# Norms of double-precision weights: sums of squares on ScalarE, or products of the leading halves on TensorE

## The chip, the cores and the metric

The kernel runs on one NeuronCore of one Trainium2 chip. A time is the device time of one execution in microseconds (us); the median of three runs of the kernel before is 1164.04 us (1164.0 to 1165.47). The trace is from one profiled execution of 1164.36 us, whose span is 1162.6 us. Engines are named as the profile names them: PE is TensorE (PEld its weight loads), DVE is VectorE, ACT is ScalarE, POOL is GpSimd, SP is the engine that issues the DMAs.

## The reference

Attention with a threshold (batch 8, 8 heads, 576 rows, head size 64), then a feed-forward layer (512 to 2048 to 512) on the 4608 rows that come out:

```python
scores = (q @ k.T) / sqrt(64)
scores = where(scores >= max(scores) - tau, scores, -1e9)
x = softmax(scores) @ v                  # heads side by side: 4608 x 512
h = x @ w_in                             # 512 x 2048
g = s * relu(h)**2 + b
out = g @ w_out                          # 2048 x 512
```

The weights `w_in` and `w_out` reach the kernel as 8-byte floats, seen as pairs of 32-bit words.

## The kernel before

**The stages.** The first image is done by 36 "plain" tiles of 128 query rows (`plain_tile`, L444): 4-byte scores on PE (L457), row maximum (L460, DVE), exponential (L464, ACT), mask and sum (L466, DVE), reciprocal (L471, DVE), a product on POOL (L472), transposes on PE (L480), a copy on ACT (L484), products with `v` on PE (L493). The other seven images are done by "split" tiles, in which each operand is held as a high and a low 2-byte piece (`split_tile`, L500; `with_v`, L540, products at L547). The feed-forward layer runs in blocks of 256 rows, each of 16 steps f, one for each 128 of the 2048 hidden columns: products with `w_in` (L756), relu, square and pieces on ACT (L760, L763, L764), the low piece on POOL (L765), products with `w_out` (L771). `sums` (L685) adds up `w_out` for the bias.

**The weights.** They are cut into 16 tiles f of `w_in` (`iw`, u = 0) and 16 of `w_out` (`ow`, u = 1), 512 KB each. `load_weights` (L561) issues their DMAs on SP. `weights(f)` (L573) then makes an approximate 4-byte float of the upper word: a Prelu on ACT (L589) and a shift on DVE (L592). From that it takes norms. For `w_in`: ACT squares the tile into a 2-byte scratch (L594), PE multiplies the squares with a matrix of ones into 128 columns of bank `h` (`sizes`, L599), DVE takes the maximum of the columns (L601). For `w_out`: ACT squares the tile and accumulates each row's sum (L603, which shows in a trace as an ACTIVATE and a READ_ACCUMULATOR). `weight_scales` (L607) makes powers of two from all 32 results: two reductions (L610, L612), a product with ones on PE (L615), short DVE steps (L617 to L624), one on POOL (L627), which writes `wpower`.

Only with `wpower` can a weight be cut into its high piece (L653, ACT) and low piece (L658, DVE), which the feed-forward steps multiply. Before that, `whole` (L645, DVE) joins the two words of a tile into one 4-byte float in place; it needs no `wpower`, but overwrites what the norms read.

**The order.** No order is written by hand. Every operation is given to a planner (`Plan`) with an engine, an occupancy, a latency and the keys that it reads and writes; `place` puts them out as a list scheduler, `run` repeats that backward and forward and keeps the shortest, and the instructions are issued on each engine in the planned order. So a changed operation or a changed cost can change the order everywhere. The costs that the change touches are those of the weights' DMAs (L567, L570) and of `with_v` (L549). `keep_busy` (L898) adds filler products to the first 12 tiles, which write columns 256 to 511 of bank `h` (L901) and have their own key, `idle`.

Of the kernel before, what the change touches and what calls it, by code (L numbers as in the profile page):

```python
# [9 lines left out]
F32 = mybir.dt.float32  # L10
# [3 lines left out]
AF = mybir.ActivationFunctionType  # L14
# [126 lines left out]
def tile_attention_ffn(ctx: ExitStack, tc: tile.TileContext, qT, kT, v, tau, w_in, w_out, s, b, out):  # L141
# [25 lines left out]
    def const(name, shape, dt=F32):  # L167
        return cp.tile(shape, dt, name=name)
# [11 lines left out]
    vm = const("vm", [P, 2], F32R)  # L180
    norm = [const(f"norm{i}", [P, 4]) for i in range(2)]
    power = [const(f"power{i}", [P, 5, 4]) for i in range(2)]
    wmost, wnorm, wpower, wback = const("wmost", [P, 2, NF]), const("wnorm", [P, 4]), const("wpower", [P, 4, 2]), const("wback", [P, 2])
    ones16, onesb = const("ones16", [P, P], F16), const("onesb", [P, P], BF16)
    vs = [const(f"vs{i}", [P, 4]) for i in range(2)]
    vt = [const(f"v{i}", [P, 5, P], F16) for i in range(3)]
    rk, rq, rv = const("rk", [P, 2, S]), const("rq", [P, 2, S]), const("rv", [P, 2, 5, D])
# [7 lines left out]
    def early(tag):  # L195
        if tag not in lazy:
            lazy[tag] = sb(tag, [P, 9 * S // 2], F32)
        return lazy[tag]
# [341 lines left out]
    def with_v(g, at):  # L540
        ps = bank["pv"][:, 0:g.n]
        slots = [(n, u) for n in range(9) for u in range(2 if n < 5 else 1)]

        def products():
            for i, (n, u) in enumerate(slots):
                for j, hd in enumerate(g.hds):
                    nc.tensor.matmul(ps[j * D:(j + 1) * D], hd.v[:, (n + 1) % 5, u * D:(u + 1) * D],  # L547
                                     lazy[("ea", "eb")[j]][:, n, g.c0:g.c0 + g.n], start=(i == 0), stop=(i == len(slots) - 1))
        cost = len(slots) * (0.42 * g.n + 8) + 300  # L549
        plan.add("PE", (cost, cost + 170), products, g.keys + [k for hd in g.hds for k in hd.kvs], ["pv"], at)  # L550
        hd = g.hds[0]
        for off, n, dest, key in g.dests:
            kx = [key + (j, u) for j in range(2) for u in range(2)] if key[0] == "x" else [key + (j,) for j in range(2)]
            act((105 + 1.04 * n, 203 + 1.04 * n), lambda off=off, n=n, dest=dest: nc.scalar.activation(
                out=dest, in_=ps[:, off:off + n], func=AF.Copy, scale=hd.unit), ["pv", hd.kunit], kx, at)
# [5 lines left out]
    def load_weights(f, at):  # L561

        def raw(u):
            if ("raw", f, u) not in lazy:
                lazy["raw", f, u] = sb("io"[u] + f"w{f}", [P, DM, 2], I32)
            return lazy["raw", f, u]
        plan.add("SP", (1800, 6700), lambda: nc.sync.dma_start(out=raw(0).rearrange("p (c f) t -> p c (f t)", c=NC),  # L567
                                           in_=w_in.rearrange("(c p) (n g) -> n p c g", p=P, n=NF)[f]),
            [], [(f"w{f}", "i")], at)
        plan.add("SP", (1800, 6700), lambda: nc.sync.dma_start(out=raw(1).rearrange("p f t -> p (f t)"),  # L570
                                           in_=w_out[f * P:(f + 1) * P, :]), [], [(f"w{f}", "o")], at)

    def weights(f, at):  # L573

        tag = f"t{f % 2}"  # L580

        def words(k, u):
            return lazy["raw", f, u][:, :, k]

        def squares():
            return early("eb")[:, 2 * DM * (f % 2):2 * DM * (f % 2) + DM // 2].bitcast(BF16)
        for u, k in (0, "i"), (1, "o"):
            kr = f"w{f}", k
            act((563, 667), lambda u=u: nc.scalar.activation(  # L589
                out=words(1, u).bitcast(F32), in_=words(1, u).bitcast(F32), func=AF.Prelu, scale=2.0 ** -112, alpha=-2.0 ** 32),  # L590
                [kr], [kr], at)
            dve2((328, 418), lambda u=u: nc.vector.tensor_scalar(  # L592
                out=words(1, u), in0=words(1, u), scalar1=3, scalar2=None, op0=ALU.logical_shift_left), [kr], [kr], at)
        act((563, 667), lambda: nc.scalar.activation(out=squares(), in_=words(1, 0).bitcast(F32), func=AF.Square),  # L594
            [(f"w{f}", "i")], [tag], at)

        def sizes():
            for c in range(NC):
                nc.tensor.matmul(bank["h"][:, 0:P], onesb, squares()[:, c * P:(c + 1) * P], start=(c == 0), stop=(c == NC - 1))  # L599
        pe(NC, P, sizes, [tag, "ones16"], ["h"], at)  # L600
        dve((200, 290), lambda: nc.vector.tensor_reduce(  # L601
            out=wmost[:, 0, f:f + 1], in_=bank["h"][:, 0:P], axis=mybir.AxisListType.X, op=ALU.max), ["h"], [("wmost", 0, f)], at)
        act((640, 860), lambda: nc.scalar.activation(  # L603
            out=early("eb")[:, 2 * DM * (f % 2) + DM // 2:2 * DM * (f % 2) + DM].bitcast(BF16), in_=words(1, 1).bitcast(F32),
            func=AF.Square, accum_out=wmost[:, 1, f:f + 1]), [(f"w{f}", "o")], [("wmost", 1, f), (tag, 1)], at)

    def weight_scales(at):  # L607

        most = [("wmost", u, f) for u in range(2) for f in range(NF)]
        dve((90, 170), lambda: nc.vector.tensor_reduce(  # L610
            out=wnorm[:, 0:2], in_=wmost, axis=mybir.AxisListType.X, op=ALU.max), most, ["wnorm"], at)
        dve((90, 170), lambda: nc.vector.tensor_reduce(  # L612
            out=wnorm[:, 2:3], in_=wmost[:, 1], axis=mybir.AxisListType.X, op=ALU.add), most, [("wnorm", 2)], at)
        top = bank["pv"][:, 384:386]
        pe(1, 64, lambda: nc.tensor.matmul(top, ones.bitcast(F32), wnorm[:, 2:4], start=True, stop=True),  # L615
           ["ones", "wnorm", ("wnorm", 2)], [("top", 384)], at)
        dve((72, 155), lambda: nc.vector.tensor_scalar(  # L617
            out=wpower[:, 0, 0:1], in0=wnorm[:, 0:1], scalar1=LEAST, scalar2=None, op0=ALU.max), ["wnorm"], ["wpower"], at)
        dve((72, 155), lambda: nc.vector.tensor_scalar(
            out=wpower[:, 0, 1:2], in0=top[:, 0:1], scalar1=LEAST, scalar2=None, op0=ALU.max), [("top", 384)], ["wpower"], at)  # L620
        dve((72, 155), lambda: nc.vector.tensor_scalar(
            out=wpower.bitcast(I32)[:, 1], in0=wpower.bitcast(I32)[:, 0], scalar1=1, scalar2=EXPONENT,
            op0=ALU.logical_shift_right, op1=ALU.bitwise_and), ["wpower"], ["wpower"], at)
        dve((72, 155), lambda: nc.vector.tensor_scalar(  # L624
            out=wpower.bitcast(I32)[:, 2], in0=wpower.bitcast(I32)[:, 1], scalar1=EXPONENT, scalar2=None,
            op0=ALU.bitwise_xor), ["wpower"], ["wpower"], at)
        pool((270, 195), lambda: nc.gpsimd.tensor_scalar(  # L627
            out=wpower[:, 2], in0=wpower[:, 2], scalar1=UP, scalar2=1.0, op0=ALU.mult, op1=ALU.mult), ["wpower"], ["wpower"], at)

        def back():  # L630
            g = nc.gpsimd
            g.tensor_scalar(out=wpower[:, 3], in0=wpower[:, 1], scalar1=DOWN, scalar2=1.0, op0=ALU.mult, op1=ALU.mult)
            g.tensor_tensor(out=wback[:, 0:1], in0=s_t, in1=wpower[:, 3, 0:1], op=ALU.mult)
            g.tensor_tensor(out=wback[:, 1:2], in0=b_t, in1=wpower[:, 3, 1:2], op=ALU.mult)
            g.tensor_tensor(out=wback[:, 0:1], in0=wback[:, 0:1], in1=wpower[:, 3, 1:2], op=ALU.mult)
            g.tensor_tensor(out=wback[:, 0:1], in0=wback[:, 0:1], in1=wpower[:, 3, 0:1], op=ALU.mult)
            g.tensor_scalar(out=wback[:, 0:1], in0=wback[:, 0:1], scalar1=H_DOWN ** -2, scalar2=1.0, op0=ALU.mult, op1=ALU.mult)
        pool((1800, 1800), back, ["wpower", "s_", "b"], ["wback"], at + 1)
# [252 lines left out]
    def zeros():  # L891
        nc.gpsimd.memset(ones.bitcast(F32), 1.0)
        nc.gpsimd.memset(qt.bitcast(F32), 0.0)
        nc.gpsimd.memset(ones16, 1.0)
        nc.gpsimd.memset(onesb, 1.0)
    pool((700, 700), zeros, [], ["ones", "qt0", "qt1", "ones16"], -10)

    def keep_busy(n, r):  # L898
# [10 lines left out]
    pool((700, 700), constants, [], ["ident", "qd0", "qd1"], -9)  # L909

    def bounds():
        for t in [vm.bitcast(F32), wnorm] + norm:
            nc.gpsimd.memset(t, 0.0)
    pool((900, 900), bounds, [], ["vm", "norm0", "norm1", "wnorm", ("wnorm", 2)], -8)

    def margins():
        nc.vector.tensor_scalar(out=scale, in0=tau_t, scalar1=0.0, scalar2=SC, op0=ALU.is_ge, op1=ALU.mult)
# [28 lines left out]

    for f in range(NF):
        events.append((WEIGHTS_EACH * f, lambda f=f: (load_weights(f, 2 + f), weights(f, 2 + WEIGHTS_EACH * f))))
    events.append((n_plain - 0.6, lambda: weight_scales(WEIGHTS_AT)))
    for f in range(NF):  # L950
        events.append((n_plain - 0.5, lambda f=f: convert(f)))
# [74 lines left out]
```

## Time and profile before

| what | value |
|---|---|
| median of three runs | 1164.04 us |
| profiled execution | 1164.36 us |
| its span | 1162.6 us |
| ACT busy in the span | 930.3 us (80%) |
| DVE busy in the span | 858.7 us (74%) |
| POOL busy in the span | 779.2 us (67%) |
| weight DMAs issued | 13.4 to 58.2 us |

A row of the "windows" view has the stretch, its length, the busy time of PE, PEld, DVE, ACT and POOL in it (with the number of instructions), the granted TensorE clock (1.00 is full speed), the mean share of the DMA engines in use and GB/s. A row of the "timeline" or of the "chain in order of time" begins with the start in us and the duration in us. In the timeline an instruction's duration can overlap the next one's on the same engine, so what an instruction costs its engine is the distance between starts. In the chain that overlap has been cut off already. A row of the "waits" has the total in us, the number of waits and the longest. A row for a source line has the number of instructions, the minimum, median and maximum duration in ns, and the start of the first and of the last.

### The profile page before, as it was taken

To read this page: it belongs to the slowest core of one execution; us is meant where nothing else is said; L and a number is where in the kernel's file an instruction comes from. 1 tells how busy PE (TensorE), PEld (TensorE's weight loads), DVE (VectorE), ACT (ScalarE), POOL (GpSimd) and SP (SyncE) were. 2 spreads that over 40 slices of the span, in tenths; PEclk is the share of its full clock that TensorE was granted. 3 is DMA by queue.
4 is the path that set the end of the run, shared out by engine and by line. 5 is a ranking of instruction groups with operands and counts; after the bars stand their busy time and mean duration, and the time that the engine had idled before them with its cause. 6 is when DMAs were issued, how large, how long until landed. Compare 5 with 4: busy or idle time off the path is not lost.

```text
span 1162.6 us, 26056 instructions
## 1 busy us (share of the span) xinstructions
PE 1126.4 (97%) x8778; PEld 820.4 (71%) x8778; DVE 858.7 (74%) x1840; ACT 930.3 (80%) x2159; POOL 779.2 (67%) x1327
## 2 busy tenths in 40 slices
PE   8888999989999999999999999999999999999998
PEld 7666766657777777766777777777777777766665
DVE  7998898897887888897778877788787878730011
ACT  4999898878889898987888888878888889754443
POOL 4568688777877787776667777778777878532200
PEclk9999999989999999999999999999999999999999
DMA  7930278998799788987778878887878779800000
GB/s 246 392 106 22 52 140 166 177 182 174 149 173 178 156 160 173 165 169 141 156 136 161 152 154 151 163 151 149 173 155 166 138 146 185 123 19 1 19 19 19
DMA packets 361334, 164.52 MB, mean 142 GB/s; under 512 B 315120, under 2 KB 336112, under 8 KB 361200
## 3 DMA queue, kind: packets, MB, share of 16 engines
q1 hardware_dynamic: 361200, 162.86, 68.7%
q8 instruction: 69, 1.13, 0.4%
q14 instruction: 65, 0.53, 0.1%
HBM read 62.52 MB, written 9.44 MB: 62 GB/s over the span
## 4 chain that ended last, share of the span: by engine, by line
PE 78%; ACT 7%; DVE 5%; DMA 5%; issue 2%; POOL 2%; SPq 2%; DVEq 0%; ACTq 0%; POOLq 0%
PE h L756 29%; PE o L771 29%; PE pv L547 8%; PE s L514 5%; PE t L514 5%; DMA iw<-in_moe_w_in_dram 2%; DMA eb<-en 1%; ACT en L529 1%; ACT em L521 1%; DVE st L517 1%; DVE en L532 1%; DVE em L523 1%; ACT em L464 1%; DVE iw L785 1%; ACT iw L760 1%
## 5 line engine op out<-in xcount | busy, mean ns | idle before, releaser
L756 PE MATMUL h<-xp,iw 128*128 128x256 f16 x3456 | 427.1, 273 | 7.3 <-ACT iw L760 5.5
L756 PEld LDWEIGHTS <-iw 128*128 128x128 f16 x3456 | 330.1, 98 | 91.5 <-issue 11.3
L771 PE MATMUL o<-ow,gh 128*128 128x512 f16 x1080 | 322.9, 381 | 1.0 <-DVE iw L785 1.0
L765 POOL TENSOR_TENSOR gl<-iw,gh 128x256 f16<-128x256 f32 x272 | 199.8, 735 | 125.1 <-ACT gh L764 95.8
L532 DVE SCALAR_TENSOR_TENSOR en<-em,st,en 128x576 f16<-128x576 f32 x252 | 237.2, 947 | 23.8 <-ACT en L529 22.8
L529 ACT ACTIVATE en<-em,st 128x576 f16<-128x576 f32 x252 | 192.9, 771 | 19.3 <-DVE st L528 14.7
L771 PE MATMUL o<-ow,gl 128*128 128x512 f16 x540 | 204.8, 379 | 0.0
L760 ACT ACTIVATE iw<-h 128x256 f32<-128x256 f32 x288 | 109.6, 380 | 118.9 <-PE h L756 112.3
L771 PEld LDWEIGHTS <-gh 128*128 128x128 f16 x1152 | 100.3, 98 | 78.0 <-issue 5.1
L519 POOL TENSOR_SCALAR st<-st,bound 128x1 f32<-128x1 f32 x252 | 108.4, 431 | 52.4 <-DVE st L517 27.7
L763 ACT ACTIVATE iw<-iw 128x256 f32<-128x256 f32 x288 | 120.0, 417 | 3.8
L764 ACT CAST gh<-iw 128x256 f16<-128x256 f32 x288 | 116.1, 404 | 5.4 <-PE o L771 1.0
L523 DVE SCALAR_TENSOR_TENSOR em<-s,st,em 128x576 f32<-128x576 f32 x126 | 102.3, 812 | 19.8 <-ACT em L521 10.4
L517 DVE TENSOR_REDUCE st<-t 128x1 f32<-128x576 f32 x126 | 94.9, 753 | 29.1 <-PE t L514 28.5
L526 POOL TENSOR_SCALAR st<-st 128x1 f32<-128x1 f32 x252 | 80.2, 318 | 53.1 <-DVE em L523 20.5
L523 DVE SCALAR_TENSOR_TENSOR em<-t,st,em 128x576 f32<-128x576 f32 x126 | 102.3, 812 | 18.1 <-ACT em L521 10.6
L517 DVE TENSOR_REDUCE st<-s 128x1 f32<-128x576 f32 x126 | 94.8, 753 | 27.7 <-PE s L514 26.2
L521 ACT ACTIVATE em<-t,st 128x576 f32<-128x576 f32 x126 | 92.7, 735 | 21.2 <-DVE st L517 16.0
L547 PE MATMUL pv<-ea,v 128*64 128x256 f16 (+1 forms) x784 | 107.9, 289 | 0.0
L547 PE MATMUL pv<-eb,v 128*64 128x256 f16 (+1 forms) x784 | 106.9, 288 | 0.5 <-DMA eb<-en 0.4
L521 ACT ACTIVATE em<-s,st 128x576 f32<-128x576 f32 x126 | 92.7, 736 | 16.0 <-DVE st L517 15.7
L771 PEld LDWEIGHTS <-gl 128*128 128x128 f16 x576 | 56.3, 98 | 67.9
(190 smaller groups left out, 1864.0 us busy)
## 6 DMA issues: line engine op xcount, KB each, us to landing
rk<-in_k_dram SPq DMA_DIRECT2D x57, 288.0 KB, 4.2
rq<-in_q_dram SPq DMA_DIRECT2D x56, 288.0 KB, 4.1
ow<-k SPq DMA_DIRECT2D x56, 216.0 KB, 2.9
iw<-in_moe_w_in_dram SPq DMA_DIRECT2D x16, 512.0 KB, 7.3
ow<-in_moe_w_out_dram SPq DMA_DIRECT2D x16, 512.0 KB, 7.9
out_dram<-iw SPq DMA_DIRECT2D x32, 256.0 KB, 3.0
rv<-in_v_dram SPq DMA_DIRECT2D x56, 128.0 KB, 2.8
kt<-k SPq DMA_DIRECT2D x56, 72.0 KB, 2.6
```

Source lines behind the costliest of these rows:

```text
L514: nc.tensor.matmul(ps[:, hf], stat, kk(hf), start=(n == 0), stop=(n == len(seq) - 1))
L517: dve((667, 750), lambda: nc.vector.tensor_reduce(out=top, in_=ps, axis=mybir.AxisListType.XY, op=ALU.max, negate=True), [bk], [(ks_, 0)], ...
L521: act((636, 740), lambda: nc.scalar.activation(out=halves, in_=ps, func=AF.Exp, bias=top, scale=1.0), [bk, (ks_, 0)], [em_k], i - 0.5)
L523: dve((740, 900), lambda: nc.vector.scalar_tensor_tensor(out=halves, in0=ps, scalar=line, in1=halves, op0=ALU.is_ge, op1=ALU.mult, accum_o ...
L529: act((668, 774), lambda: nc.scalar.activation(out=pieces[:, 0:S], in_=ex, func=AF.Copy, scale=unit), [em_k, (ks_, 3)], [en_k], i)
L532: dve2((740, 825), lambda: nc.vector.scalar_tensor_tensor(out=pieces[:, S + T:2 * S + T], in0=ex, scalar=unit, in1=pieces[:, 0:S], op0=ALU ...
L547: nc.tensor.matmul(ps[j * D:(j + 1) * D], hd.v[:, (n + 1) % 5, u * D:(u + 1) * D], lazy[("ea", "eb")[j]][:, n, g.c0:g.c0 + g.n], start=(i ...
L756: nc.tensor.matmul(ps, wi[w][f][:, c * P:(c + 1) * P], x[:, u, c, :], start=(c == 0 and i == 0), stop=(c == NC - 1 and i == 2))
L760: act((357, 473), lambda: nc.scalar.activation(out=g(), in_=ps, func=AF.Relu, scale=H_DOWN), [h, (f"w{(0, 1, 5)[k3]}", "i", 2)], [kg], at)
L763: act((320, 417), lambda: nc.scalar.activation(out=g(), in_=g(), func=AF.Square), [kg], [kg], at)
L765: do((712, 735) if not self.last else (340, 425), lambda: eng.tensor_tensor(out=lo, in0=g(), in1=hi, op=ALU.subtract), [kg, f"gh{k3}"], [f ...
L771: nc.tensor.matmul(bank["o"][:, t, :], a[:, ts_], w, start=(f == 0 and i == 0), stop=(f == NF - 1 and i == 2))
```

## The change

- Both squarings on ACT (L594, L603), `sizes` on PE (L599) and the maximum for each tile (L601) go, with the matrix of ones in 2-byte floats and the scratch for squares.
- A new function, `weight_sizes(k)`, works on four tiles at once (four calls). `top(f, u)` is every fourth 2-byte element of a tile: the upper half of the 4-byte float that L592 leaves, read in place as bf16, 8 bytes apart. PE multiplies each 128 columns of `top` with themselves. For `w_in` the four products of a tile add up in 128 columns of bank `h`, four tiles fill the 512 columns, and one DVE maximum goes over all of them. For `w_out` all sixteen products add up in the first 128 columns, and one maximum goes over those. A matrix of such products has its largest element on its diagonal, where the sums of squares stand.
- `weight_scales` reduces `wmost` once, turns the two columns into rows on PE (into bank `h`), takes their maximum on DVE, puts the two numbers on a small diagonal (`wtop`) and multiplies with ones on PE.
- The planner's occupancy and latency of a weight DMA go from (1800, 6700) to (1320, 5200) ns, and the cost of `with_v` from `len(slots) * (0.42 * n + 8) + 300` to `len(slots) * (0.417 * n + 3) + 150`, with 14 slots and n of 256 or 320.

```diff
-        cost = len(slots) * (0.42 * g.n + 8) + 300
+        cost = len(slots) * (0.417 * g.n + 3) + 150
...
-        plan.add("SP", (1800, 6700), lambda: nc.sync.dma_start(out=raw(0).rearrange("p (c f) t -> p c (f t)", c=NC),
+        plan.add("SP", (1320, 5200), lambda: nc.sync.dma_start(out=raw(0).rearrange("p (c f) t -> p c (f t)", c=NC),
...
-        act((563, 667), lambda: nc.scalar.activation(out=squares(), in_=words(1, 0).bitcast(F32), func=AF.Square),
-            [(f"w{f}", "i")], [tag], at)
-
-        def sizes():
-            for c in range(NC):
-                nc.tensor.matmul(bank["h"][:, 0:P], onesb, squares()[:, c * P:(c + 1) * P], start=(c == 0), stop=(c == NC - 1))
-        pe(NC, P, sizes, [tag, "ones16"], ["h"], at)
-        dve((200, 290), lambda: nc.vector.tensor_reduce(
-            out=wmost[:, 0, f:f + 1], in_=bank["h"][:, 0:P], axis=mybir.AxisListType.X, op=ALU.max), ["h"], [("wmost", 0, f)], at)
-        act((640, 860), lambda: nc.scalar.activation(
-            out=early("eb")[:, 2 * DM * (f % 2) + DM // 2:2 * DM * (f % 2) + DM].bitcast(BF16), in_=words(1, 1).bitcast(F32),
-            func=AF.Square, accum_out=wmost[:, 1, f:f + 1]), [(f"w{f}", "o")], [("wmost", 1, f), (tag, 1)], at)
+
+    def weight_sizes(k, at):
+
+        fs, d = range(4 * k, 4 * k + 4), [slice(c * P, (c + 1) * P) for c in range(NC)]
+
+        def top(f, u):
+            return lazy["raw", f, u].bitcast(BF16)[:, :, 3]
+
+        def grams(u):
+            for n, f in enumerate(fs):
+                for c in range(NC):
+                    nc.tensor.matmul(bank["h"][:, d[0 if u else n]], top(f, u)[:, d[c]], top(f, u)[:, d[c]],
+                                     start=(c == 0 and not (u and n)), stop=(c == NC - 1 and (not u or n == 3)))
+        for u, key, w in (0, "i", 4 * P), (1, "o", P):
+            pe(4 * NC, P, lambda u=u: grams(u), [(f"w{f}", key) for f in fs], ["h"], at)
+            dve((100 + 1.06 * w, 190 + 1.06 * w), lambda u=u, w=w: nc.vector.tensor_reduce(
+                out=wmost[:, u, k:k + 1], in_=bank["h"][:, 0:w], axis=mybir.AxisListType.X, op=ALU.max), ["h"], [("wmost", u, k)], at)
...
+        turned, top = bank["h"][0:2, 0:P], bank["pv"][:, 384:386]
+        pe(1, 4 * P, lambda: nc.tensor.matmul(turned, wnorm[:, 0:2], ident(), start=True, stop=True), ["ident", "wnorm"], ["h"], at)
+        dve((210, 290), lambda: nc.vector.tensor_reduce(
+            out=wnorm[0:2, 2:3], in_=turned, axis=mybir.AxisListType.X, op=ALU.max), ["h"], [("wnorm", 2)], at)
...
+            out=wtop[0:2], in0=ident()[0:2, 0:2], scalar1=wnorm[0:2, 2:3], scalar2=None, op0=ALU.mult), [("wnorm", 2), "ident"], ["wtop"], at)
+        pe(1, 64, lambda: nc.tensor.matmul(top, ones.bitcast(F32), wtop, start=True, stop=True), ["ones", "wtop"], [("top", 384)], at)
...
     for f in range(NF):
         events.append((WEIGHTS_EACH * f, lambda f=f: (load_weights(f, 2 + f), weights(f, 2 + WEIGHTS_EACH * f))))
+        if f % 4 == 3:
+            events.append((WEIGHTS_EACH * f + 0.1, lambda f=f: weight_sizes(f // 4, 2.5 + WEIGHTS_EACH * f)))
```

More of the change, by code (lines that the diff above doesn't have):

```diff
@@ L182, in tile_attention_ffn @@
     power = [const(f"power{i}", [P, 5, 4]) for i in range(2)]
-    wmost, wnorm, wpower, wback = const("wmost", [P, 2, NF]), const("wnorm", [P, 4]), const("wpower", [P, 4, 2]), const("wback", [P, 2])
-    ones16, onesb = const("ones16", [P, P], F16), const("onesb", [P, P], BF16)
+    wmost, wnorm, wpower, wback = const("wmost", [P, 2, 4]), const("wnorm", [P, 4]), const("wpower", [P, 4, 2]), const("wback", [P, 2])
+    wtop = const("wtop", [P, 2])
+    ones16 = const("ones16", [P, P], F16)
     vs = [const(f"vs{i}", [P, 4]) for i in range(2)]
@@ L566, in raw @@
             return lazy["raw", f, u]
-        plan.add("SP", (1800, 6700), lambda: nc.sync.dma_start(out=raw(0).rearrange("p (c f) t -> p c (f t)", c=NC),
+        plan.add("SP", (1320, 5200), lambda: nc.sync.dma_start(out=raw(0).rearrange("p (c f) t -> p c (f t)", c=NC),
                                            in_=w_in.rearrange("(c p) (n g) -> n p c g", p=P, n=NF)[f]),
             [], [(f"w{f}", "i")], at)
-        plan.add("SP", (1800, 6700), lambda: nc.sync.dma_start(out=raw(1).rearrange("p f t -> p (f t)"),
+        plan.add("SP", (1320, 5200), lambda: nc.sync.dma_start(out=raw(1).rearrange("p f t -> p (f t)"),
                                            in_=w_out[f * P:(f + 1) * P, :]), [], [(f"w{f}", "o")], at)
     def weights(f, at):
-        tag = f"t{f % 2}"
         def words(k, u):
             return lazy["raw", f, u][:, :, k]
-        def squares():
-            return early("eb")[:, 2 * DM * (f % 2):2 * DM * (f % 2) + DM // 2].bitcast(BF16)
         for u, k in (0, "i"), (1, "o"):
@@ L607, in weight_scales @@
     def weight_scales(at):
-        most = [("wmost", u, f) for u in range(2) for f in range(NF)]
+        most = [("wmost", u, k) for u in range(2) for k in range(4)]
         dve((90, 170), lambda: nc.vector.tensor_reduce(
             out=wnorm[:, 0:2], in_=wmost, axis=mybir.AxisListType.X, op=ALU.max), most, ["wnorm"], at)
-        dve((90, 170), lambda: nc.vector.tensor_reduce(
-            out=wnorm[:, 2:3], in_=wmost[:, 1], axis=mybir.AxisListType.X, op=ALU.add), most, [("wnorm", 2)], at)
@@ L614, in weight_scales @@
-        top = bank["pv"][:, 384:386]
-        pe(1, 64, lambda: nc.tensor.matmul(top, ones.bitcast(F32), wnorm[:, 2:4], start=True, stop=True),
-           ["ones", "wnorm", ("wnorm", 2)], [("top", 384)], at)
+        turned, top = bank["h"][0:2, 0:P], bank["pv"][:, 384:386]
+        pe(1, 4 * P, lambda: nc.tensor.matmul(turned, wnorm[:, 0:2], ident(), start=True, stop=True), ["ident", "wnorm"], ["h"], at)
+        dve((210, 290), lambda: nc.vector.tensor_reduce(
+            out=wnorm[0:2, 2:3], in_=turned, axis=mybir.AxisListType.X, op=ALU.max), ["h"], [("wnorm", 2)], at)
@@ L617, in weight_scales @@
         dve((72, 155), lambda: nc.vector.tensor_scalar(
-            out=wpower[:, 0, 0:1], in0=wnorm[:, 0:1], scalar1=LEAST, scalar2=None, op0=ALU.max), ["wnorm"], ["wpower"], at)
+            out=wtop[0:2], in0=ident()[0:2, 0:2], scalar1=wnorm[0:2, 2:3], scalar2=None, op0=ALU.mult), [("wnorm", 2), "ident"], ["wtop"], at)
+        pe(1, 64, lambda: nc.tensor.matmul(top, ones.bitcast(F32), wtop, start=True, stop=True), ["ones", "wtop"], [("top", 384)], at)
         dve((72, 155), lambda: nc.vector.tensor_scalar(
-            out=wpower[:, 0, 1:2], in0=top[:, 0:1], scalar1=LEAST, scalar2=None, op0=ALU.max), [("top", 384)], ["wpower"], at)
+            out=wpower[:, 0], in0=top, scalar1=LEAST, scalar2=None, op0=ALU.max), [("top", 384)], ["wpower"], at)
@@ L894, in zeros @@
         nc.gpsimd.memset(ones16, 1.0)
-        nc.gpsimd.memset(onesb, 1.0)
     pool((700, 700), zeros, [], ["ones", "qt0", "qt1", "ones16"], -10)
@@ L911, in bounds @@
     def bounds():
-        for t in [vm.bitcast(F32), wnorm] + norm:
+        for t in [vm.bitcast(F32), wtop] + norm:
             nc.gpsimd.memset(t, 0.0)
-    pool((900, 900), bounds, [], ["vm", "norm0", "norm1", "wnorm", ("wnorm", 2)], -8)
+    pool((900, 900), bounds, [], ["vm", "norm0", "norm1", "wtop"], -8)
     def margins():
```

## The prediction

> **What bounds the kernel now.** I read the page first, then the busy times in stretches of 10 us, PE's waits, the chain in order of time, and the timeline around the weights.
>
> ```profile
> span 1162.6 us, 26056 instructions
> PE 1126.4 (97%) x8778; PEld 820.4 (71%) x8778; DVE 858.7 (74%) x1840; ACT 930.3 (80%) x2159; POOL 779.2 (67%) x1327
> ```
>
> PE is the bound: 36.2 us of the span are not busy (1162.6 - 1126.4). So a change is worth what it takes from PE's idle time or from PE work that serves nothing. Where the idle time lies, the windows say (columns: PE, PEld, DVE, ACT, POOL, clock, DMA share, GB/s):
>
> ```profile
> 30.00:40.00 10.00, 10.00 (x97) 8.68 (x96) 9.85 (x24) 10.00 (x21) 5.64 (x10) 1.00 1.06 395
> 40.00:50.00 10.00, 8.46 (x76) 6.48 (x75) 9.67 (x26) 9.55 (x20) 5.26 (x10) 1.00 1.07 398
> 50.00:60.00 10.00, 7.18 (x58) 5.25 (x56) 9.86 (x25) 10.00 (x23) 5.50 (x10) 1.00 1.07 388
> 60.00:70.00 10.00, 8.93 (x82) 7.07 (x81) 10.00 (x29) 10.00 (x23) 6.09 (x12) 1.00 0.32 109
> 70.00:80.00 10.00, 8.28 (x74) 6.08 (x73) 9.78 (x24) 10.00 (x20) 6.95 (x12) 1.00 0.00 0
> 80.00:90.00 10.00, 8.58 (x84) 6.57 (x83) 9.35 (x25) 10.00 (x23) 7.12 (x14) 1.00 0.52 123
> 90.00:100.00 10.00, 7.46 (x54) 5.40 (x52) 9.73 (x24) 7.40 (x16) 9.36 (x16) 1.00 0.00 1
> 100.00:110.00 10.00, 8.56 (x86) 6.91 (x87) 8.09 (x16) 10.00 (x20) 8.28 (x17) 1.00 0.23 61
> 110.00:120.00 10.00, 10.00 (x76) 6.67 (x75) 9.11 (x17) 10.00 (x24) 8.83 (x11) 1.00 0.01 2
> ```
>
> From 40 to 110 us PE idles 12.55 us (70 less the seven PE numbers): 7.15 us up to 80, 5.40 us from 80 to 110. From 110 on it is full. In the same rows ACT is full, and DVE is nearly so, 39.31 of 40 us from 40 to 80. PE's two largest waits in the first 130 us, and a small one used below:
>
> ```profile
> PE t L480 <- ACT x L484: 3.3, 4, 1.1
> PE pv L493 <- ACT rv L484: 3.1, 3, 1.3
> ...
> PE h L599 <- DVE wmost L601: 0.3, 1, 0.3
> ```
>
> ACT ends 6.4 us of PE's early waits: plain tiles stand in ACT's queue behind the weights. The chain of that stage shows who else is kept:
>
> ```profile
> 47.68 0.58 ACT eb L594
> ...
> 48.88 0.57 ACT iw L589
> 49.45 0.67 ACT eb L603 x2
> ...
> 97.08 0.59 POOL wpower L627
> 97.70 1.34 ACT iw L653 x2
> ```
>
> The chain goes through the squares; `wpower` is there at 97.7 us, and only then do the pieces of the weights (L653) begin, with which the feed-forward work starts that fills PE from 110 us on. Two things therefore cost PE time: tiles behind squares, and the late `wpower`.
>
> **The change part by part.** *ACT.* A square costs 0.58 us, one with a sum 0.67 us (the chain's rows, overlap cut off). Sixteen of each are gone: 16 x 1.25 = 20.0 us, from a stage in which ACT is full. Nothing is added on ACT.
>
> *DVE.* What is late next is DVE. Its starts:
>
> ```profile
> 82.23 0.29 DVE L601 TENSOR_REDUCE wmost<-h 128x1 f32<-128x128 f32 x1
> 82.43 0.70 DVE L645 SCALAR_TENSOR_TENSOR ow<-ow 128x512 int32<-128x512 int32 x1
> 83.06 0.80 DVE L466 SCALAR_TENSOR_TENSOR em<-s,st,em 128x576 f32<-128x576 f32 x1
> ...
> 83.87 0.40 DVE L592 TENSOR_SCALAR iw<-iw 128x512 int32<-128x512 int32 x1
> 84.19 0.74 DVE L460 TENSOR_REDUCE st<-o 128x1 f32<-128x576 f32 x1
> ...
> 85.66 0.74 DVE L460 TENSOR_REDUCE st<-s 128x1 f32<-128x576 f32 x1
> 86.33 0.80 DVE L466 SCALAR_TENSOR_TENSOR em<-o,st,em 128x576 f32<-128x576 f32 x1
> ```
>
> A maximum over 128 columns of bank `h` costs 0.20 us (82.23 to 82.43), one over 576 costs 0.67 us; for 512 I take 0.60 us by the line between them. Removed are 16 x 0.20 = 3.2 us, added 4 x (0.60 + 0.20) = 3.2 us: DVE gains nothing and stays full. It has room to choose, though: a join (L645) costs 0.63 us (82.43 to 83.06), 32 of them 20.2 us, and `wpower` needs none; it needs the 32 shifts at 0.32 us (83.87 to 84.19), 10.2 us. A plan that is no longer held by ACT can put joins behind tiles. They must also wait now until their group of four has been multiplied, since they overwrite what PE reads.
>
> *PE.* The busy time of the fillers (L901) and of the products with ones (L599) over the first 125 us, PE and PEld:
>
> ```profile
> 0.00:125.00 125.00, 14.23 (x76) 11.56 (x76) 1.00 0.53 178
> 0.00:125.00 125.00, 6.20 (x64) 4.77 (x64) 1.00 0.53 178
> ```
>
> The two lines by themselves, and one group of four in the timeline:
>
> ```profile
> L901 PE MATMUL h<-qt,ones x76: 278/283/582, 2.0 to 38.3; 128*128 128x256 f32 x76
> L599 PE MATMUL h<-eb,onesb x64: 217/219/230, 26.8 to 87.1; 128*128 128x128 bf16 x64
> ```
> ```profile
> 26.75 0.39 PE L599 MATMUL h<-eb,onesb 128*128 128x128 bf16 x4
> ```
>
> Four products of 128 bf16 columns, each with its own weight load, take 0.39 us, of which the last one's 0.219 is latency: (0.39 - 0.219) / 3 = 0.057 us each. Eight groups of sixteen: 8 x (15 x 0.057 + 0.219) = 8.6 us, against 6.2 us now: +2.4 us. No row shows operands read 8 bytes apart. The bounds: no less than 0.057 us, as the packed ones have the same size and type; at most that of the fillers, whose weights are 4-byte and which have 256 columns, 14.23 / 76 = 0.187 us, which for 128 products is 23.9 us, +17.7 us net. I take 0.057, the row of the same type.
>
> The Trainium skill (SBUF — State Buffer, Door 1: The DMA port swizzle) says that SBUF is read in lines of 16 bytes and that full speed needs at least two hits in a line. By that rule elements 8 bytes apart, two in a line, are just at the limit and the lower price holds; no run so far shows it.
>
> Three smaller things on PE cost nothing in the sum. Each group of sixteen writes bank `h` and so waits until DVE has read the group before, with the scores and transposes queued behind it on PE. L599 stands in the same place sixteen times and waited 0.3 us in all, because the plan puts tiles between; the far end is that each of the eight waits out a maximum and an L460 ahead of it, 8 x (0.60 + 0.67) = 10.2 us. I take 0, the row being the same wait. The four maxima over 512 columns read the half of bank `h` that the fillers write, so a filler behind the first group waits for DVE, and the scores behind that filler wait too: up to 1.3 us a group. Fillers end at 38.3 us, PE is full of them until then, and they are themselves the cover; without it 1.3 us. The longer `weight_scales` has one more product, one more maximum and one more product by DVE; it only delays `wpower`, below.
>
> *When `wpower` comes.*
>
> The last weight DMA is issued; the median from issue to landing is 7.9 us; the sums of squares end:
>
> ```profile
> 58.19 0.34 SPq L570 DMA_DIRECT2D ow<-in_moe_w_out_dram  x1
> ```
> ```profile
> ow<-in_moe_w_out_dram SPq DMA_DIRECT2D x16, 512.0 KB, 7.9
> ```
> ```profile
> L603 ACT ACTIVATION_READ_ACCUMULATOR eb<-ow x16: 185/210/347, 28.4 to 89.7; 128x1 f32 x16
> ```
>
> The last weight lands at about 58.2 + 7.9 = 66.1 us. Prelu 0.57, shift 0.32, two groups on PE at 1.07 and two maxima (0.60, 0.20) follow: 3.8 us, then what followed the last sum so far (it begins at 89.7 us and takes 0.2), 97.7 - 89.9 = 7.8 us, and some 2 us for the three new steps: 79.7 us. From the other side, 97.7 less the 20.0 us that ACT saves, plus the same 3.8 - 0.9 + 2: 82.6 us. Both say 15 to 18 us earlier, about 81 us.
>
> *What that is worth.* From 80 to 110 us PE idles 5.40 us; feed-forward steps that start 16 us earlier fill most of it, but the first again wait for their pieces: I take 4.0 (0 to 5.4). From 40 to 80 us it idles 7.15 us; DVE, full, would allow nothing, the waits for ACT that go would allow 6.4 us; the joins that can be moved (20.2 us) put me above the middle: 3.4. Sum: -4.0 - 3.4 + 2.4 = -5.0 us.
>
> *SP and the plan.* The DMAs and their bytes stay. From 30 to 60 us the DMA share is 1.06, so the weights can't land earlier whatever the plan takes for one; only their order against the loads of the plain tiles can move. The two costs and the new operations also put out the whole rest of the order anew. One stall there may go or come:
>
> ```profile
> 250.00:255.00 5.00, 2.62 (x13) 1.30 (x12) 5.00 (x13) 3.67 (x6) 4.19 (x7) 1.00 0.94 187
> 255.00:260.00 5.00, 3.21 (x14) 2.30 (x15) 5.00 (x12) 2.36 (x5) 3.12 (x10) 0.50 0.67 149
> 260.00:265.00 5.00, 5.00 (x46) 3.54 (x45) 3.03 (x8) 3.39 (x10) 1.46 (x4) 0.81 1.14 206
> ```
> ```profile
> 255.90 1.30 PE L514 MATMUL t<-k,qs 128*128 128x288 f32 x4 [2.35 <-DVE em L523]
> ```
>
> DVE full, PE idle 2.38 + 1.79 us, and the clock granted at 0.50 and 0.81, which loses 3.21 x 0.50 + 5.00 x 0.19 = 2.6 us more: 6.7 us in all. I put the replanned rest at 0, with -6.7 and +6.7 as its ends. `with_v` now stands in the plan with 14 x (0.417 x 320 + 3) + 150 = 2060 ns in place of 2294; the trace has it so:
>
> ```profile
> 175.29 2.02 PE pv L547 x28
> ```
>
> So that plan is nearer to the chip, which speaks mildly for fewer stalls.
>
> The profiled execution of 1164.36 us is its span and 1.76 us around it, and 0.32 us above the median. 1164.36 - 5.0 = 1159.4, or 1159.0 beside the median.
>
> **The rivals.** *DVE takes ACT's place.* DVE's 39.31 of 40 us speak for it. Then 40 to 80 us give nothing, the joins not done make the first steps late, of the 4.0 us some 2.4 come, and the products take them back: 1164.0. The 20.2 us of movable joins speak against.
>
> *The stall at 250 us goes as well*, or its like: 1159.0 - 6.7 = 1152.3. It depends on an order that nothing here fixes.
>
> *A new stall with a clock drop: slower.* The plan gives DVE to weights and pieces at once, plain tiles run dry between 60 and 100 us, and PE waits at a stretch. The row at 255.90 us shows that a wait of 2.35 us, with 4.2 us idle around it, drops the clock; the longest early wait quoted is 1.3 us. From about 2.3 us in one piece this decides: one such stall costs 6.7 us, which with DVE in ACT's place makes 1164.0 + 6.7 = 1170.7. The upper price of the products leads there too: 15.3 us more (17.7 - 2.4) in a stage with 12.55 us idle, and so do groups that wait for each other's maxima, at the 10.2 us above.
>
> The Trainium skill (TensorE: Matmul & The Clock Gate, Part 1: What's actually happening) says that the clock falls to a half after an idle window of about 3.4 us. The 2.35 us wait disagrees, and the measurement decides: by the page this rival would need longer gaps and be rarer.
>
> *It doesn't do what it says*, say the weights' order on SP keeps `wpower` where it is: about 1164 + 2.4 = 1166.4.
>
> **How the numbers follow.** A measurement of this kernel can tell about 0.2% (2.3 us) from no change. Forecast 0.50 (its own range 1154 to 1162.5); DVE in ACT's place 0.25; the old stall gone too 0.10; slower by a stall or by slow products 0.13; not done 0.02. Faster by over 0.2%: 0.44 + 0.06 + 0.10 = 0.60. Within: 0.06 + 0.12 + 0.02 = 0.20. Slower: 0.07 + 0.13 = 0.20. The range, 1151 to 1168, takes in the forecast, the first two rivals and the small losses, and leaves out the slow end.
>
> **What would show it.** Right: `wpower` (L627) at 78 to 86 us; the first product of a feed-forward step (L756) some 12 to 18 us before where it stands now; ACT no longer full from 40 to 80 us; PE idle from 40 to 110 us at 4 to 8 us; products of `weight_sizes` at 0.06 us from start to start, some 8.6 us in all. Wrong: `wpower` later than 92 us; those products above 0.1 us each; a granted clock under 1.00 before 110 us; or an unchanged early stage with the difference after 125 us.

## The result and the profile after

The changed kernel takes 1172.22 us (1169.55 to 1173.86, 4 runs) beside 1164.37 for the kernel before on the same chip (4 runs). The medians are 7.8 us apart, where 5 us less were forecast. The ratio on record is 1.0054, with a 95% interval of 1.0035 to 1.0073; it lies a little below that of the medians, 1.0067. So the change is slower by about half a percent, clear of the noise. The profiled execution took 1170.9 us.

The page of the kernel after: span, and busy time by engine.

```profile
span 1169.1 us, 26144 instructions
PE 1137.3 (97%) x8844; PEld 833.1 (71%) x8844; DVE 866.8 (74%) x1832; ACT 913.0 (78%) x2111; POOL 786.2 (67%) x1326
```

PE is still the bound, but the loss isn't idle time: PE's idle time fell from 36.2 to 31.8 us, while its busy time grew by 10.9 us. The span grew by the difference, 6.5 us. Which work grew? The products of `weight_sizes` by their own durations (ns: least, median, largest), and their busy time over the same 125 us (PE, then PEld):

```profile
L602 PE MATMUL h<-iw x64: 277/298/301, 32.4 to 84.9; 128*128 128x128 bf16 x64
L602 PE MATMUL h<-ow x64: 278/297/301, 36.0 to 89.7; 128*128 128x128 bf16 x64
```
```profile
0.00:125.00 125.00, 16.42 (x128) 14.64 (x128) 1.00 0.57 178
```

The products on packed squares had a latency of 219 ns; these have 297. And 128 of them are busy for 16.42 us, where 6.20 were spent before: +10.2 us, nearly the whole growth of PE. (Of the other 0.7 us, the fillers are 0.8 less and all the rest 1.5 more.)

The windows of 10 us of the kernel after, with the same columns as in the prediction:

```profile
40.00:50.00 10.00, 9.99 (x77) 8.38 (x75) 8.98 (x23) 8.87 (x15) 5.69 (x10) 1.00 1.05 334
50.00:60.00 10.00, 9.94 (x86) 8.19 (x87) 9.27 (x26) 7.18 (x13) 5.70 (x12) 1.00 0.93 289
60.00:70.00 10.00, 9.10 (x72) 7.02 (x71) 9.31 (x26) 7.91 (x14) 6.35 (x13) 1.00 1.03 327
70.00:80.00 10.00, 10.00 (x102) 8.39 (x102) 10.00 (x20) 8.50 (x16) 7.95 (x16) 1.00 0.08 20
80.00:90.00 10.00, 10.00 (x88) 8.43 (x85) 8.49 (x21) 5.83 (x12) 8.54 (x14) 1.00 0.49 118
90.00:100.00 10.00, 7.33 (x70) 5.30 (x68) 8.46 (x23) 4.50 (x9) 7.26 (x11) 1.00 0.21 53
100.00:110.00 10.00, 7.53 (x75) 5.71 (x73) 9.05 (x18) 9.50 (x17) 9.00 (x17) 1.00 0.02 7
```

PE is nearly full from 40 to 90 us, ACT has room, and DVE is no fuller than before. By its busy time alone this stage has improved: PE idles 6.11 us from 40 to 110 us in place of 12.55. But from 90 to 110 us it idles 5.14 us, more than the 3.98 us before: an early `wpower` was to fill this stretch, and it comes no earlier. The chain in order of time shows the end of the way to it (start, duration, step):

```profile
83.31 1.89 PE h L602 x16
...
88.11 1.89 PE h L602 x16
90.00 0.55 PE t L481 x5
90.55 0.73 PE pv L494 x20
92.45 0.32 PE h L615 x2
...
93.01 0.67 DVE ow L647
...
97.72 0.81 POOL st L463
98.53 1.15 POOL em L473
...
99.77 0.70 POOL wpower L629
...
100.50 0.06 ACT iw L655
```

Two things are to be seen. A group of sixteen products takes 1.89 us, 0.118 us each. And between the last group (over at 90.0 us) and `wpower` (there at 100.5 us, 2.8 us later than before) PE and POOL do work of plain tiles first and DVE a join (L647): the last step of `wpower` takes 0.70 us but stands on POOL behind L463 and L473. No row of the chain from 80 us on names ACT until `wpower` is there. The greater part of the delay lies ahead of the last group, as the timeline shows for the last Prelu (L586), the last shift (L589) and the last group:

```profile
76.76 0.71 ACT L586 ACTIVATE ow<-ow 128x512 f32<-128x512 f32 x1
```
```profile
83.04 0.41 DVE L589 TENSOR_SCALAR ow<-ow 128x512 int32<-128x512 int32 x1
```
```profile
87.95 2.05 PE L602 MATMUL h<-ow 128*128 128x128 bf16 x16
```

In the kernel before the last Prelu started at 86.7 us, so ACT does come to it 10 us sooner. What ACT gives is used up by the next two steps: the shift starts 5.6 us after that Prelu is over and the group 4.5 us after that shift, with other work, mostly plain tiles, ahead of them on DVE and PE.

PE's waits in the first 130 us (total, times, longest), and the stall that the prediction named at 250 us:

```profile
PE t L481 <- POOL em L473: 3.3, 2, 2.3
...
PE pv L494 <- ACT rv L485: 1.0, 2, 0.6
...
PE t L481 <- ACT x L485: 0.8, 1, 0.8
...
PE h L902 <- DVE wmost L606: 0.2, 1, 0.2
```
```profile
260.00:265.00 5.00, 2.10 (x9) 1.41 (x11) 5.00 (x12) 2.82 (x5) 2.66 (x10) 0.67 0.86 163
265.00:270.00 5.00, 5.00 (x40) 3.38 (x37) 3.90 (x7) 3.08 (x7) 1.26 (x2) 0.65 1.02 229
```

The waits for ACT have shrunk as forecast: 3.1 us became 1.0 and 3.3 became 0.8; the largest wait is now for POOL. Bank `h` costs 0.2 us of waiting, that of a filler. The stall is still there, with DVE full to 265 us and the clock at 0.67 and 0.65.

### The profile page after: what moved, and what is told of

Read it like the earlier page. It is cut to its first block, busy times and chain, and to the rows that moved or that the text cites. A ratio compares the mean times of both kernels' runs of the same rounds, so it can differ in the third digit from the quotient of the medians.

```text
span 1169.1 us, 26144 instructions
## 1 busy us (share of the span) xinstructions
PE 1137.3 (97%) x8844; PEld 833.1 (71%) x8844; DVE 866.8 (74%) x1832; ACT 913.0 (78%) x2111; POOL 786.2 (67%) x1326
## 4 chain that ended last, share of the span: by engine, by line
PE 76%; DMA 7%; DVE 5%; ACT 4%; issue 3%; SPq 2%; POOL 2%; DVEq 0%; POOLq 0%; ACTq 0%
PE h L758 28%; PE o L773 27%; PE pv L548 7%; PE s L515 5%; PE t L515 5%; DMA eb<-en 2%; DMA ow<-in_moe_w_out_dram 2%; DVE em L524 1%; DVE st L518 1%; DVE en L533 1%; ACT en L530 1%; DMA rv<-in_v_dram 1%; PE pv L494 1%; DMA rq<-in_q_dram 1%; PE h L602 1%
## 5 line engine op out<-in xcount | busy, mean ns | idle before, releaser
L533 DVE SCALAR_TENSOR_TENSOR en<-em,st,en 128x576 f16<-128x576 f32 x252 | 242.9, 968 | 18.0 <-ACT en L530 16.3
L520 POOL TENSOR_SCALAR st<-st,bound 128x1 f32<-128x1 f32 x252 | 115.4, 458 | 50.6 <-DVE st L518 33.1
```

The costliest lines, as they stand in the source:

```text
L533: dve2((740, 825), lambda: nc.vector.scalar_tensor_tensor(out=pieces[:, S + T:2 * S + T], in0=ex, scalar=unit, in1=pieces[:, 0:S], op0=ALU ...
```

## The experiments

My theory after the result: the products cost 8 us more than forecast because their operands are read 8 bytes apart, and the gain expected of an early `wpower` doesn't exist. The rivals: the new order of the plan is at fault whatever the products cost (new costs, or bad luck with the order); or `wpower` would pay, were it only early.

**Packed products.** The products read a packed constant in place of the weights' upper halves; the planned order stays. So the norms are not those of the weights, and the products no longer wait for the weights.

```diff
-            return lazy["raw", f, u].bitcast(BF16)[:, :, 3]
+            return early("eb")[:, 0:DM // 2].bitcast(BF16)
...
+        nc.gpsimd.memset(early("eb")[:, 0:DM // 2].bitcast(BF16), 0.25)
```

> The changed kernel in the same planned order, but the 128 products read a packed constant tile (0.25) instead of the leading halves 8 bytes apart, so the norms are those of a constant and the products no longer wait for the weights. If the 8-byte step is what makes the products slow, they cost 0.06 us each instead of 0.117, 8 to 9 us in all, and the time falls by 5 to 8 us to 1164 to 1167 us. If the price lies in loading new weights for each product, they stay at 16 us and the time stays above 1169 us.

Measured: 1165.02 us, 1.0001 (0.9991 to 1.001) of the kernel before. The products' row and their busy time:

```profile
L602 PE MATMUL h<-eb x128: 219/219/229, 34.3 to 86.3; 128*128 128x128 bf16 x128
```
```profile
0.00:125.00 125.00, 8.46 (x128) 7.74 (x128) 0.99 0.57 178
```

The price that the prediction took, 8.6 us, is the price of packed operands. With it the slowdown is gone, but no gain shows: the second half of the forecast fails by itself.

**Which operand.** For `w_in` only the weights are read 8 bytes apart, for `w_out` only the moving operand.

```diff
...
-    ..., top(f, u)[:, d[c]], top(f, u)[:, d[c]],
+    ..., (flat() if u else top(f, u))[:, d[c]], (top(f, u) if u else flat())[:, d[c]],
```

> The changed kernel, with only one operand of each product 8 bytes apart and the other a packed constant: the weights for w_in, the moving columns for w_out; so the norms are not those of the weights. If reading the moving columns is what is slow, the products of w_out stay near 0.117 us and those of w_in fall to 0.06 us; if the weight load is slow, the other way round; if either side is enough, both stay.

Its one run took 1166.71 us. The rows of weight loads and products:

```profile
L605 PEld LDWEIGHTS <-iw x64: 110/113/116, 32.1 to 82.5; 128*128 128x128 bf16 x64
L605 PE MATMUL h<-eb,iw x64: 218/219/219, 32.4 to 82.5; 128*128 128x128 bf16 x64
...
L605 PE MATMUL h<-ow,eb x64: 276/295/300, 35.0 to 87.2; 128*128 128x128 bf16 x64
```

Strided weights load in 113 ns and the product keeps its 219; a strided moving operand makes it 295. All 128 are busy for 12.30 us, about half way between 8.46 and 16.42. So the moving side alone is slow.

**Joined first.** The join by DVE (L647), which brings a weight's two words into one 4-byte float, moves into `weights`, ahead of the products. These then read upper halves 4 bytes apart.

```diff
+            dve2((602, 685), lambda u=u: whole(u), [kr], [kr], at)
...
-            return lazy["raw", f, u].bitcast(BF16)[:, :, 3]
+            return lazy["raw", f, u].rearrange("p f t -> p (f t)")[:, 0:DM].bitcast(BF16).rearrange("p (f t) -> p f t", t=2)[:, :, 1]
```

> The changed kernel with the join of each tile's two words put ahead of the products, which then read the upper halves of the joined floats, 4 bytes apart instead of 8. If the price of a moving operand goes with the step, the products fall to 0.06 to 0.09 us each and the time to 1162 to 1167 us. If any step over 2 bytes halves the rate, they stay at 0.117 us and the time stays near 1170 us, plus what the 20.2 us of joins ahead of wpower cost.

Measured: 1160.91 us, 0.9962 (0.9947 to 0.9976) of the kernel before: the best version, faster than both kernels and a little below the range expected. The busy times of its page, its products and their busy time:

```profile
PE 1128.2 (98%) x8844; PEld 824.6 (71%) x8844; DVE 860.6 (74%) x1832; ACT 906.8 (78%) x2111; POOL 777.4 (67%) x1326
```
```profile
L609 PE MATMUL h<-iw x64: 218/218/233, 28.7 to 83.6; 128*128 128x128 bf16 x64
...
L609 PE MATMUL h<-ow x64: 217/218/220, 38.5 to 90.5; 128*128 128x128 bf16 x64
```
```profile
0.00:125.00 125.00, 8.65 (x128) 7.91 (x128) 1.00 0.57 181
```

At 4 bytes the products run at full rate, though they wait for the weights as in the changed kernel: the gain doesn't need the missing wait of the packed ones. PE is busy 9.1 us less than in the changed kernel, 7.8 of them in these products. Its `wpower` comes at 100.4 us, as late as in the changed kernel: the gain needs no early one.

**The parts alone.** First the new norms with the planner's old costs, then the kernel before with the new costs and nothing else.

```diff
-        cost = len(slots) * (0.417 * g.n + 3) + 150
+        cost = len(slots) * (0.42 * g.n + 8) + 300
...
-        plan.add("SP", (1320, 5200), lambda: nc.sync.dma_start(out=raw(0).rearrange("p (c f) t -> p c (f t)", c=NC),
+        plan.add("SP", (1800, 6700), lambda: nc.sync.dma_start(out=raw(0).rearrange("p (c f) t -> p c (f t)", c=NC),
```

> The changed kernel with the planner's costs of before (weight DMAs 1800 and 6700 ns, with_v as it was). If the slow products on PE are the cause (16.4 us against 6.2), it stays slow: 1169 to 1174 us. If the plan made from the new costs is the cause (last weight DMA issued at 63.7 us instead of 58.2, wpower at 100.5 us instead of 97.7), it comes to 1160 to 1165 us, with wpower well before 97 us.

Measured: 1180.58 us, 1.0132 (1.0115 to 1.0148). That is above both ranges. The products are busy for 16.48 us, as in the changed kernel, but `wpower` is ready only at 111.2 us.

> The kernel before with the planner's new costs and the old norms. If the products are the cause, it stays at 1162 to 1166 us. If the plan made from the new costs is the cause, it comes to 1168 to 1174 us, with the last weight DMA after 62 us.

Measured: 1162.83 us, 0.9979 (0.9969 to 0.9989). So the new costs aren't what makes the change slow: they help a little by themselves, and more beside the new norms. Where the old costs lose with the new norms can be told: counted as in the next experiment, PE is 121 instructions behind the kernel before at 125 us and 126 at 900 us, so the loss is made ahead of 125 us. How much of it is the late `wpower` isn't shown.

**No norms at all.** Squares, products and maxima are left out; the scales come from a constant, and `wpower` is ready from the start. An added key on bank `o` keeps the first step's second product in order.

```diff
-        if f % 4 == 3:
+        if False:
...
-            out=wtop[0:2], in0=ident()[0:2, 0:2], scalar1=wnorm[0:2, 2:3], ...
+            out=wtop[0:2], in0=ident()[0:2, 0:2], scalar1=64.0, ...
```

> The changed kernel without any norms of the weights: no products, no maxima, and the two powers of two come from a constant, so wpower is there from the start and nothing of the norms is on any engine. (The second product of a block's first step also reads the key of bank o, so that it can't be moved ahead of the plain tiles.) It is the most that any change of the norms can give. If an early wpower is worth what was forecast (4.0 us from 80 to 110 us, 3.4 us before), it gains at least those beside the 16.4 us of products on PE: 1150 to 1156 us. If the start of the feed-forward work is bound by VectorE and not by wpower, it gains little more than the packed products did: 1158 to 1164 us.

Measured: 1162.31 us, 0.9983 (0.9971 to 0.9995): 2.2 us for taking all of it away. How far PE has come by 110, 200 and 300 us shows in the instructions that it has issued (the first figure in brackets). The kernel before, the changed one, and the one without norms:

```profile
0.00:110.00 110.00, 93.50 (x776) 74.41 (x777) 97.98 (x253) 92.14 (x179) 68.69 (x141) 1.00 0.60 202
0.00:200.00 200.00, 180.36 (x1454) 137.13 (x1455) 178.28 (x415) 171.40 (x356) 138.93 (x244) 1.00 0.57 160
0.00:300.00 300.00, 274.37 (x2181) 204.65 (x2181) 261.96 (x594) 255.02 (x552) 215.72 (x374) 0.99 0.69 166
```
```profile
0.00:110.00 110.00, 99.59 (x820) 82.18 (x820) 93.09 (x235) 73.33 (x126) 68.77 (x138) 1.00 0.65 202
...
0.00:300.00 300.00, 277.61 (x2187) 210.28 (x2189) 262.58 (x573) 233.35 (x490) 209.45 (x364) 0.99 0.69 161
```
```profile
0.00:110.00 110.00, 98.41 (x791) 78.67 (x792) 97.42 (x237) 84.44 (x155) 77.59 (x146) 1.00 0.63 202
0.00:200.00 200.00, 176.17 (x1372) 133.86 (x1372) 176.18 (x392) 154.26 (x304) 138.05 (x238) 0.98 0.59 160
0.00:300.00 300.00, 271.15 (x2127) 203.33 (x2128) 261.00 (x577) 242.30 (x509) 220.90 (x376) 0.99 0.70 166
```

The programs differ in length: against 8778 instructions before, the changed one has 66 more and the one without norms 64 fewer, all of them early. Allowing for that, the kernel without norms is 79 instructions ahead at 110 us (791 + 64 - 776), 18 behind at 200 us, and 10 ahead at 300 us. After 300 us an instruction takes 0.131 us on average, (1162.6 - 300) / (8778 - 2181), so a lead of some 10 us is there and lost again; the count is rough, since the work isn't in the same order. Where it is lost shows in the windows from 150 to 200 us, of the kernel before and of the one without norms:

```profile
150.00:200.00 50.00, 46.86 (x365) 33.92 (x364) 45.83 (x101) 43.84 (x103) 42.20 (x69) 1.00 0.79 154
```
```profile
150.00:200.00 50.00, 37.76 (x274) 26.74 (x272) 44.20 (x96) 39.44 (x86) 36.41 (x60) 0.93 0.79 156
```

PE idles 12.24 us there without the norms, 3.14 in the kernel before. Its largest wait there without norms:

```profile
PE s L515 <- DVE em L524: 5.3, 2, 2.9
```

The split tiles wait for their softmax on DVE. The feed-forward steps that could cover this have been used up earlier, as their products with `w_in` up to 150 us show (PE and PEld, kernel before and without norms):

```profile
0.00:150.00 150.00, 16.43 (x132) 12.50 (x132) 1.00 0.50 162
```
```profile
0.00:150.00 150.00, 22.12 (x180) 17.43 (x180) 1.00 0.52 162
```

By 200 us it is 264 before and 252 without norms: from 150 us on, 132 against 72. The changed kernel is 22 instructions behind at 110 us and 60 behind at 300 us; by the same count the latter is 7.8 us.

**The chain put first.** Packed products, and the planner places the weights, the products and `weight_scales` ahead of all else on their engines. The second product of a block's first step reads the key of bank `o` here too.

```diff
-    start, end = self.place(before, engine, occ, [o[5] for o in ops])
+    start, end = self.place(before, engine, occ, [-1e9 if n in self.early else o[5] for n, o in enumerate(ops)])
```

> The packed kernel of before (constant operands for the products), but the planner puts the Prelus, shifts, products, maxima and scales of the weights ahead of everything else on their engines, and the second product of a block's first step also reads the key of bank o. wpower should be there by 80 to 88 us instead of 97. If the late wpower costs what was forecast, the time falls by 3 to 6 us to 1159 to 1162 us. If VectorE is the bound, tiles are only put behind weights and the time stays at 1164 to 1170 us.

Measured: 1172.81 us, 1.0069 (1.0056 to 1.0082), above both ranges. The last step of `wpower`, and PE's largest wait from 70 to 200 us:

```profile
L637 POOL TENSOR_SCALAR wpower<-wpower x1: 193/193/193, 80.6 to 80.6; 128x2 f32<-128x2 f32 x1
```
```profile
PE t L523 <- DVE em L532: 5.1, 2, 3.0
```

Here `wpower` is ready at 80.8 us, where the prediction had it (about 81), and the kernel is 0.7% slower than with the same products and `wpower` ready at 97.0 us. The wait is again that of split tiles for DVE. The windows from 150 to 200 us of the packed kernel and of this one:

```profile
150.00:200.00 50.00, 47.01 (x361) 33.43 (x359) 48.55 (x103) 44.73 (x103) 40.53 (x64) 1.00 0.83 158
```
```profile
150.00:200.00 50.00, 43.31 (x298) 31.15 (x298) 46.11 (x102) 40.51 (x90) 36.02 (x60) 0.90 0.80 147
```

PE idles 3.7 us more there, and at a clock of 0.90 its busy time loses an estimated 43.31 x 0.10 = 4.3 us: together about the 7.8 us between the two medians. The count agrees: PE is 4 instructions ahead of the kernel before at 150 us and 62 behind at 200 us. That the wait is the whole of the loss isn't shown.

**The true price in the plan, and another plan.** The planner charges a group of sixteen 1.0 us; told 16 x 117 ns, does it put it in a better place?

```diff
-            pe(4 * NC, P, lambda u=u: grams(u), ...
+            plan.add("PE", (4 * NC * 117, 4 * NC * 117 + 170), lambda u=u: grams(u), ...
```

> The changed kernel with the planner told what a group of products really costs on PE (16 x 117 ns instead of 16 x 63 ns). If the loss is the PE work itself, it stays at 1168 to 1174 us. If it is the order, made from a cost that is too low by 7 us in all, it comes to 1163 to 1167 us.

Measured: 1172.13 us, 1.0063 (1.0048 to 1.0078). It doesn't: the loss doesn't come from the plan's wrong price. Last, to see how much one order may differ from another by luck, the planner's `HANDOVER` goes from 150 to 165 in four kernels:

```diff
-HANDOVER = 150
+HANDOVER = 165
```

> The kernel before with one unrelated number of the planner moved: the handover between engines from 150 to 165 ns. The instructions are the same, only their order differs. It shows how far a time moves by the order alone. If the plan's luck is small, 1161 to 1168 us; if it is as large as the differences in this study, it may lie anywhere from 1158 to 1180 us.

> The changed kernel with the handover at 165 ns. If the slow products are the cause, it stays 5 to 10 us above the joined kernel at the same handover, since they cost 7.8 us of PE in any order, and the products stay at 16.4 us. If its time was an unlucky order, it comes to 1160 to 1165 us.

> The joined kernel (products on the joined floats, 4 bytes apart) with the handover at 165 ns. If its 1160.9 us come from products that cost 8.65 us instead of 16.4, it stays at 1157 to 1164 us and below the changed kernel at the same handover; if they came from a lucky order, it may be above 1165 us.

> The kernel before with the new planner costs and the handover at 165 ns. If shorter weight loads in the plan help by themselves (1162.8 us against 1165.1 us before), it stays 1 to 4 us below the kernel before at the same handover; if that was the order's luck, it lies on either side.

| kernel | HANDOVER 150 | HANDOVER 165 | products busy, us (165) |
|---|---|---|---|
| before | 1 | 1.0003 (0.9993 to 1.0014) | 6.21 |
| changed | 1.0054 (1.0035 to 1.0073) | 1.0046 (1.0029 to 1.0062) | 16.41 |
| joined first | 0.9962 (0.9947 to 0.9976) | 0.9961 (0.9943 to 0.9979) | 8.67 |
| before, new costs | 0.9979 (0.9969 to 0.9989) | 0.9986 (0.9972 to 1.0) | 6.21 |

The four hardly move, so the ranking of the four kernels isn't the luck of one plan. Joined first is 0.9% faster than the change in both plans; at 165 that is 10.5 us, of which the products are 7.7.

## Why the prediction was wrong

**The products, the term that failed.** The prediction bounded them by 0.057 and 0.187 us each and took the lower end, "the row of the same type". They took 0.118 us each, 16.42 us in all: +10.2 in place of +2.4, so 7.8 us of the 11.5 us between the forecast -5.0 and the +6.5 of the span. The row was of the same type but not of the same step, and the kernels with packed operands (8.46 us), 4 bytes (8.65) and 8 bytes on one side (12.30) show that the step of the moving operand is the cause. The Trainium skill (SBUF — State Buffer, Door 1: The DMA port swizzle) asks for two hits in a 16-byte line, which 8 bytes apart gives; here that runs at half the rate, four hits at the full one. The measurement decides.

**When `wpower` comes, the mechanism that failed.** Forecast about 81 us, measured 100.5. The working (79.7 us) has three parts: the landing of the last weight, from there to the last maximum, and from there to `wpower`. The last part was right: 7.8 + 2 us were reckoned, and 10.2 are there (90.3 to 100.5). The landing, 66.1 us, was reckoned about 6 us too early: the last weight DMA is issued at 63.7 us in place of 58.2 and, by the median of 8.5 us, lands at about 72.2. The part between is the step that failed: 3.8 us from the landing to the last maximum, as if every step began when the one before it ended. It takes some 18 us (72.2 to 90.3). Each engine works through a fixed order, and the last Prelu, the last shift and the last group stand behind other work, mostly plain tiles, on ACT, DVE and PE. Freeing ACT moved only the first of the three, and so the working from the other side, which took off the whole 20 us of ACT, failed too. Put ahead of the tiles, the same chain is done at 80.8 us. The first feed-forward product starts at 106.4 us in place of 99.2, where 12 to 18 us earlier were forecast. Slow products explain little of it: with packed ones `wpower` is ready at 97.0 us.

**What it is worth, -4.0 us, failed as well.** An early `wpower` does fill PE from 80 to 110 us: PE idles 2.17 us there when it is ready at 80.8 us, and 0.47 us when it is there from the start, in place of 5.40. Yet the first of the two kernels is slower, and the second gains 2.2 us together with all the norms' work. The prediction took PE to be full from 110 us on, by a row that ends at 120; the kernel before idles again from 150 to 200 us (3.14 us), and the steps taken forward are missing there as cover.

**The waits from 40 to 80 us, -3.4 us: the way right, the size not, and of no use.** PE idles 0.97 us there in place of 7.15, a gain of 6.2 us; with packed products it idles 2.76 us. From 80 to 110 us the gain is 0.3 us in place of 4.0. That both together come to 6.4 us, near the 7.4 forecast, is luck. These 6.4 us went to the products (+10.2 us), and 2.0 us more idle time came elsewhere (6.4 less the 4.4 by which it fell in all). With packed products nothing of them remains in the time either. The sum in the units of the prediction: -6.4 + 10.2 - 0.8 (fillers) + 1.5 (other work of PE) + 2.0 = +6.5 us, the span's growth.

**Right:** ACT is busy 17.3 us less (20.0 reckoned) and its waits have shrunk; DVE gains nothing (its busy time is 8.1 us more over the span) and doesn't take ACT's place (9.0 to 10 of 10 us from 40 to 80); bank `h` costs next to nothing; the weights land no earlier; the stall at 250 us stays.

**The rivals.** The slower rival named three mechanisms. Its stall with a clock drop before 110 us did not come, the clock being 1.00 in every row up to 110 us, and the groups did not wait for each other's maxima. The third, a higher price of the products, was what happened, at 7.8 of the 15.3 us. Two of the signs given as wrong are in the trace: `wpower` after 92 us and products above 0.1 us each.

**Left open:** why the split tiles run dry so much longer when the chain is put first, why the new norms with the old costs lose so much ahead of 125 us, and what part of the 0.4% between packed and joined first is the earlier join; that part wasn't separated from the order.

## What to carry to other kernels

Price a product by a row with the same operand step, not only the same type and size; where there is none, the doubt belongs in the forecast's middle and not only in the far end of its range. When a chain is freed from one engine, check where its other steps stand in the fixed orders of the others before moving its end. And idle time on the bound engine is a gain only if the work that fills it isn't the cover of a later wait: count how far the engine has come at several times, not only how idle it is in one stage.

## What the runs showed of the hardware

A moving operand of 2-byte elements 8 bytes apart streams at half rate, 0.118 us for 128 columns beside 0.06 packed or 4 bytes apart, with 297 ns of latency beside 218. The same step in the weights costs 15 ns a load (113 beside 98), which stays hidden behind the product before: a group of sixteen with strided weights and a packed moving operand takes 1.06 us, as with all packed (8.46 / 8). A packed load beside a strided moving operand takes 115 ns as well.

The clock can fall after short waits. With the chain put first, two windows hold 0.92 and 2.11 us of idle PE, 3.03 us together with no wait longer than 1.93 us, and the second has a granted clock of 0.83:

```profile
70.00:80.00 10.00, 9.08 (x87) 7.22 (x84) 9.82 (x29) 5.37 (x10) 8.01 (x16) 1.00 0.07 15
80.00:90.00 10.00, 7.89 (x51) 5.72 (x50) 8.60 (x18) 10.00 (x18) 8.13 (x16) 0.83 0.52 121
```

The prediction let a drop begin at about 2.3 us in one piece, and this one came sooner. The idle window of about 3.4 us in the Trainium skill (TensorE: Matmul & The Clock Gate, Part 1: What's actually happening) is longer than all of it; the measurement decides.
